# When a batch's rows are scattered: six indirect DMAs of GpSimd moved to later units, in the first two of four batches

## The chip, the cores and the metric

One core of a Trainium2 chip runs the whole program in one launch. The metric is the device time of one execution in microseconds (us), lower is better. The kernel before takes 246.15 us, the median of three runs (246.1 to 246.69).

## The reference, cut to what matters

An attention with selected key chunks over 4 batches of 8 heads, 768 positions and 64 dimensions feeds a mixture of experts: every one of the 3072 rows goes through a dense two-layer network, and through the one of 8 experts that its gate prefers.

```
ub = sum(max(q*k_min, q*k_max))            # bound of each 32-key chunk, causal
top_chunks = argsort(ub)[..., -6:]         # six chunks for each query
scores = where(selected and causal, q@k.T / 8, -1e9)
attn = exp(scores - max); attn /= sum
x = (attn @ v) reshaped to (3072, 512)
y = relu(x @ w1_dense) @ w2_dense
e = argmax(x @ w_gate);  g = softmax(x @ w_gate)[e]
y[rows of e] += g * (relu(x[rows of e] @ w1[e]) @ w2[e])
```

## The kernel before

The attention is worked off in 16 pairs of heads (pair 0 to 15; four pairs are a batch of 768 rows), and each pair in 11 units (unit 0 to 10). A unit is a group of score tiles with up to 512 columns: TensorE multiplies (L604 in `scores`, tile `sp`), ScalarE takes the exponential (L608, tile `ex`), and where the tiles lie on the diagonal, in units 0, 5 and 6, GpSimd zeroes what is not causal with an affine select (L610, called a mask here). TensorE then multiplies `ex` with the values (L623 in `av`, tile `op`). Score tiles have three PSUM buffers.

The main loop `for i, (p, u) in enumerate(seq)` writes in each step: the scores of the unit two steps on, preparations for later pairs, the work of an earlier batch that is due in this step, and the product with the values of the unit before. Preparations are: `prep_k` (k is transposed, ScalarE copies it to `kp`, VectorE reduces it at L546 and makes `kb` at L549), `prep_q`, `prep_kt` (VectorE copies `kp` to `kT`, L553 and L554), `prep_ub` (bounds, and the flags `fl` at L584) and `prep_s` (TensorE transposes the flags at L590, tile `ps`). In unit 0 GpSimd casts v of a later pair (L535) and issues one or two expert weight loads (`we`, L214), in unit 7 it casts k and q (L528, L530).

When a batch of four pairs is done, `batch_fills(b)` lists its routing and its dense layer as small closures, and a table `at` gives each a number n. The closure with number n is run in step n + 1 of the next batch's 44 steps, so n = 0 to 9 falls in its first pair, 10 to 20 in its second, and so on. `ranks` (n = 15) computes on TensorE and VectorE the row `slot` of the table at which each token will lie (L308). `place(t)`, for t = 0 to 5, scatters 128 rows of `xbig` to the DRAM tensor `table` by an indirect DMA which GpSimd issues (L388, called a placing here); the first one also copies the row numbers into `xbig` (L382). `xbig` has two buffers, used by turns by the batches, so VectorE's first normalised rows (L634) of the batch after next wait until the six placings of this one have landed. The expert blocks of the tail read `table` after the attention.

Each engine takes its instructions in the order in which they are queued. A placing is held behind the last mask written before it (`issue_after(latest["pool"].ins)`), and a scheduler settles the rest of the order. Batch 0 is placed during pairs 5 to 7, batch 1 during pairs 9 to 11, batch 2 during pairs 13 to 15, and batch 3 in the tail, where `at` is not used.

Of the kernel before, what the change touches and what calls it, by code (L numbers as in the profile page):

```python
# [17 lines left out]
def kernel(  # L18
# [13 lines left out]
    B, H, S, D = q.shape  # L32
    NT = S // 128
# [220 lines left out]
    def batch_fills(b):  # L254
# [122 lines left out]
        def place(t):  # L377

            def f():
                with tc.issue_after(latest["pool"].ins):  # L380
                    if t == 0:
                        nc.gpsimd.tensor_copy(xbig[b % 2][:, :, Dm + 2 : Dm + 4].bitcast(mybir.dt.int32),  # L382
                                              num[:, b * NT : (b + 1) * NT])
                    put(t)
            return f

        def put(t):
            sc = nc.gpsimd.indirect_dma_start(  # L388
                out=table, out_offset=bass.IndirectOffsetOnAxis(ap=keep["slot"][:, t : t + 1], axis=0),
                in_=xbig[b % 2][:, t].bitcast(U16), in_offset=None)  # L390
            apart(sc, "rows", "every token has a row of its own")
            latest["put"] = sc
            if b == B - 1:
                tc.declare_no_dep(sc.ins, group="full", reason="the first blocks were full before this batch")
# [56 lines left out]
        at = {}  # L451
        for n, f in zip((0, 2, 4, 6, 8, 10) + (12,), out_list):
            at.setdefault(n, []).append(f)
        at.setdefault(15, []).append(ranks)
        for t in range(NT):
            at.setdefault(18 + 3 * t, []).append(place(t))
        for n, f in zip((7, 8, 9, 10, 12, 13, 14, 15, 17, 18, 19, 20, 22, 23, 24, 25, 27, 28, 29, 30, 32, 33, 34, 35, 37, 38, 39, 40), dense):
            at.setdefault(n, []).append(f)
        return out_list, dense, ranks, [place(t) for t in range(NT)], at
# [56 lines left out]
    with (  # L516
# [239 lines left out]
        def finish(p, u):  # L756
            av(p, u)
            for g in range(2):
                if u == done[g]:
                    norm(p, g)  # L760
            if u == NU - 1:
                if p % HP == HP - 1 and p + 1 < NP:
                    fills.clear()
                    fills.update(batch_fills(p // HP)[-1])
# [74 lines left out]
    with (  # L839
# [6 lines left out]
        cur.update(tr=(p1, "tr"), h=(p2, "h"), y=(p3, "y"), rk=(p4, "rk"))  # L846
        assert not fills
        a, d, ranks, places, _ = batch_fills(B - 1)

        w2f = we2.rearrange("p e j f -> p (e j f)")  # L850
# [145 lines left out]
```

## Time and profile before

| | |
|---|---|
| median of three runs | 246.15 us |
| the profiled execution: its time / its span | 247.56 us / 245.9 us |
| attention, from the start to the last masks | about 161 us |
| busy share of the span | TensorE 86%, VectorE 71%, ScalarE 71%, GpSimd 66% |
| mean granted TensorE clock | 0.983 |
| masks (L610) | 48, 667 ns each (median) |
| placings (L388) | 24, 984 ns each (median) |

The profile lists for an engine when each instruction ran, and in brackets how long the engine had stood idle before it and what ended that. [...] A wait put down to "issue" is one whose releaser the profile doesn't show.

### The profile page before, as it was taken

How to read it: one execution, taken by the hardware profiler on the slowest of the kernel's cores; microseconds unless marked ns; L12 is line 12 of the kernel's file. 1: busy time of each engine (PE TensorE's matmuls, PEld its weight loads, DVE VectorE, ACT ScalarE, POOL GpSimd, SP SyncE). 2: the span in 40 equal slices, each digit the busy share in tenths (PEclk: the TensorE clock that was granted, in tenths of full speed). 3: DMA queues.
4: the chain of work that ended last, by engine and by line, in shares of the span. 5: the costliest groups of instructions: out<-in, count | busy, mean ns of one | idle time of the engine just before them, and what ended most of it. 6: DMA issues, size and time to landing. Idle time of an engine off the chain costs nothing.

```text
span 245.9 us, 7890 instructions
## 1 busy us (share of the span) xinstructions
PE 211.6 (86%) x2771; PEld 149.6 (61%) x2771; DVE 175.4 (71%) x561; ACT 174.3 (71%) x325; POOL 162.9 (66%) x213
## 2 busy tenths in 40 slices
PE   1688878898997999988999996989999989999950
PEld 0466556676666676755667764667666557777720
DVE  3889999999989789797798996577723335555510
ACT  4579797897887898696899786644556556666630
POOL 6457997785379687268877517330688757888881
PEclk9999999999999999999999998899999999999996
DMA  6999999999899999979999946147589999968785
GB/s 174 247 268 279 210 240 251 270 214 265 222 168 358 182 300 261 263 128 251 296 177 256 188 82 182 42 119 197 157 267 215 222 250 254 204 130 122 88 122 106
DMA packets 68279, 50.55 MB, mean 206 GB/s; under 512 B 29712, under 2 KB 61328, under 8 KB 68240
## 3 DMA queue, kind: packets, MB, share of 16 engines
q1 hardware_dynamic: 53008, 30.72, 47.0%
q0 software_dynamic: 15232, 19.32, 45.8%
q8 instruction: 23, 0.38, 0.6%
q14 instruction: 16, 0.13, 0.2%
HBM read 41.93 MB, written 18.23 MB: 245 GB/s over the span
## 4 chain that ended last, share of the span: by engine, by line
PE 35%; POOL 16%; DVE 14%; issue 12%; ACT 10%; DMA 10%; POOLq 1%; SPq 0%; DVEq 0%; ACTq 0%
ACT ex L608 6%; PE yp L886 6%; PE hp L865 6%; PE hp L408 5%; POOL ex L610 4%; DMA out_dram<-yo,xg 4%; DVE ks L546 4%; PE sp L604 4%; POOL table L388 4%; PE yp L424 4%; DMA xg<-table 2%; PE op L623 2%; DMA qf<-in_q_dram 2%; ACT kp L543 2%; PE tp L856 2%
## 5 line engine op out<-in xcount | busy, mean ns | idle before, releaser
L608 ACT ACTIVATE ex<-sp 128x512 f16<-128x512 f32 (+1 forms) x176 | 91.5, 613 | 10.3 <-PE sp L604 8.5
L604 PE MATMUL sp<-rT,kT 128*128 128x128 f16 (+3 forms) x384 | 64.3, 262 | 4.3 <-ACT ex L608 1.1
L610 POOL TENSOR_SCALAR_AFFINE_SELECT ex<-ex 128x512 f16<-128x512 f16 x48 | 32.4, 685 | 37.7 <-ACT ex L608 25.6
L895 POOL DMA_INDIRECT out_dram<-yo,xg x27 | 44.8, 1660 | 12.0 <-issue 5.2
L623 PE MATMUL op<-v,ex 128*128 128x65 f16 x672 | 45.9, 194 | 7.2 <-POOL ex L610 5.6
L623 PEld LDWEIGHTS <-ex 128*128 128x128 f16 x672 | 35.9, 98 | 23.1 <-POOL ex L610 10.0
L388 POOL DMA_INDIRECT table<-xbig,slot x24 | 24.3, 1012 | 18.5 <-issue 18.5
L858 DVE COPY exT<-tp 128x512 f16<-128x512 f16 x28 | 11.8, 423 | 32.8 <-PE tp L856 31.5
L604 PEld LDWEIGHTS <-kT 128*128 128x128 f16 x384 | 28.5, 98 | 8.4 <-issue 5.2
L886 PE MATMUL yp<-we,ehT 128*128 x112 | 30.9, 379 | 0.4 <-ACT ys L429 0.2
L865 PEld LDWEIGHTS <-w 128*128 128x128 f16 x432 | 26.4, 98 | 7.9 <-issue 2.2
L408 PE MATMUL hp<-xT,wd 128*128 128x384 f16 x128 | 30.2, 341 | 0.6 <-DVE xT L264 0.6
L865 PE MATMUL hp<-exT,w 128*128 128x128 f16 x432 | 29.2, 219 | 0.7 <-issue 0.7
L893 ACT ACTIVATE yo<-yp,xg 128x512 f32<-128x512 f32 x27 | 18.5, 687 | 14.0 <-PE yp L886 13.2
L546 DVE TENSOR_REDUCE ks<-kp 128x24 f16<-128x768 f16 x28 | 25.5, 945 | 3.7 <-ACT kp L543 3.5
L424 PE MATMUL yp<-wd,hT 128*128 128x512 f16 x96 | 25.7, 379 | 0.3
L868 ACT ACTIVATE ehT<-hp 128x512 f16<-128x512 f32 x28 | 16.7, 597 | 12.1 <-PE hp L865 9.0
L413 ACT ACTIVATE hT<-hp 128x384 f16<-128x384 f32 x30 | 15.0, 498 | 12.0 <-PE hp L408 11.4
L513 DVE COPY w<-we 128x2048 f16 x27 | 18.7, 693 | 0.2 <-DVE exT L858 0.2
L634 DVE TENSOR_TENSOR xbig<-op,rs 128x384 f16<-128x384 f32 x32 | 17.5, 547 | 0.3
L429 ACT COPY ys<-yp 128x512 f32<-128x512 f32 x21 | 12.8, 609 | 6.3 <-PE yp L424 6.0
L886 PEld LDWEIGHTS <-ehT 128*128 128x128 f16 x112 | 10.2, 97 | 10.3 <-issue 3.6
(158 smaller groups left out, 371.6 us busy)
## 6 DMA issues: line engine op xcount, KB each, us to landing
we<-in_moe_w_dram POOLq DMA_DIRECT2D x16, 512.0 KB, 6.6
kf<-in_k_dram SPq DMA_DIRECT2D x32, 192.0 KB
qf<-in_q_dram SPq DMA_DIRECT2D x32, 192.0 KB
vf<-in_v_dram SPq DMA_DIRECT2D x32, 192.0 KB
out_dram<-ys SPq DMA_DIRECT2D x48, 128.0 KB
xg<-table SPq DMA_DIRECT2D x27, 136.0 KB
table<-zt SPq DMA_DIRECT2D x9, 136.0 KB
wd<-in_moe_w_dense_dram POOLq DMA_DIRECT2D x2, 512.0 KB, 6.3
```

Source lines behind the costliest of these rows:

```text
L388: sc = nc.gpsimd.indirect_dma_start(out=table, out_offset=bass.IndirectOffsetOnAxis(ap=keep["slot"][:, t : t + 1], axis=0), in_=xbig[b % 2 ...
L408: nc.tensor.matmul(hp, wd[:, ko, j * 128 : (j + 1) * 128], xT[:, ko, g * G * 128 : (g + 1) * G * 128], start=(ko == 0), stop=(ko == NK - 1))
L424: nc.tensor.matmul(yp, hold["h"][:, j, i * 128 : (i + 1) * 128], wd[:, NK + j], start=(j == 0), stop=(j == NK - 1))
L513: nc.vector.tensor_copy(w.rearrange("p j f -> p (j f)"), w1f[:, bass.ds(offs1[i], NK * 512)])
L546: nc.vector.tensor_reduce(out=ks[:, i], in_=kp.rearrange("d (c w) -> d c w", w=32), op=op, axis=mybir.AxisListType.X)
L604: last = nc.tensor.matmul(sp[:, o : o + w], kT[p % NB][g][:, kt * 128 : (kt + 1) * 128], rT[p % NB][g][:, a * 128 : z * 128], start=(o == ...
L608: scored.append((last, nc.scalar.activation(ex[:, 0:o], sp[:, 0:o], AF.Exp, scale=-0.125)))
L610: latest["pool"] = nc.gpsimd.affine_select(out=ex, in_=ex, compare_op=ALU.is_ge, fill=0.0, base=0, pattern=[[0, 4], [1, 2], [2, 64]], chan ...
L623: nc.tensor.matmul(s["op", g][:, t * (D + 1) : (t + 1) * (D + 1)], ex[:, o : o + 128], v16[p % NB][:, g, kt, :], start=first, stop=(last_o ...
L865: nc.tensor.matmul(hp[:, j], s["w1"][:, ko, j * 128 : (j + 1) * 128], s["xT"][:, ko], start=(ko == 0), stop=(ko == NK - 1), skip_group_che ...
L886: nc.tensor.matmul(yp, s["hT"][:, j], w2f[:, bass.ds(offs[i] + j * 512, 512)], start=(j == 0), stop=(j == NK - 1))
L895: sc = nc.gpsimd.indirect_dma_start(out=out, out_offset=to, in_=o, in_offset=None, bounds_check=N - 1, oob_is_err=False, compute_op=ALU.by ...
```

## The change

In `batch_fills` the placings of the first two batches get the numbers 25, 26, 30, 33, 36 and 37; they had 18, 21, 24, 27, 30 and 33. Batch 2 keeps those, batch 3 was never on the table. Each placing is thus written 4 to 7 units later, and no instruction is added or removed.

```
-        for t in range(NT):
-            at.setdefault(18 + 3 * t, []).append(place(t))
+        for t, n in enumerate((25, 26, 30, 33, 36, 37) if b < B - 2 else range(18, 36, 3)):
+            at.setdefault(n, []).append(place(t))
```

What follows is GpSimd's queue during batch 1's placings, in pair 10, from the two weight loads (`we`) behind the cast of v, to the mask of unit 0 of pair 11. `table<-xbig,slot` is a placing, and the AFFINE_SELECT rows are the masks. Before:

```order
L214 DMA we_176<-in_moe_w2_dram 128x4x512 x2
L388 DMA table<-xbig_172,slot 25728x544 x2
L610 AFFINE_SELECT ex<-ex 128x512
L388 DMA table<-xbig_172,slot 25728x544
L610 AFFINE_SELECT ex<-ex 128x512
L388 DMA table<-xbig_172,slot 25728x544
L528 CAST k_2806<-kf 128x768
L530 CAST q_2808<-qf 128x768
L610 AFFINE_SELECT ex<-ex 128x512
```

And now, for the same stretch:

```order
L214 DMA we_176<-in_moe_w2_dram 128x4x512 x2
L610 AFFINE_SELECT ex<-ex 128x512 x2
L382 COPY xbig_172<-num 128x6
L528 CAST k_2804<-kf 128x768
L388 DMA table<-xbig_172,slot 25728x544 x2
L530 CAST q_2806<-qf 128x768
L610 AFFINE_SELECT ex<-ex 128x512
```

The masks of units 5 and 6 stand ahead of all placings, where three stood ahead of or between them; two placings now stand between the casts of k and q.

The next stretch of the same queue runs from that mask to the mask of unit 0 of pair 12. Before:

```order
L388 DMA table<-xbig_172,slot 25728x544 x2
L535 CAST v_1_119<-vf 128x12x64
L214 DMA we_176<-in_moe_w2_dram 128x4x512 x2
L610 AFFINE_SELECT ex<-ex 128x512 x2
L528 CAST k_3034<-kf 128x768
L530 CAST q_3036<-qf 128x768
L610 AFFINE_SELECT ex<-ex 128x512
```

And now:

```order
L388 DMA table<-xbig_172,slot 25728x544 x2
L535 CAST v_1_119<-vf 128x12x64
L214 DMA we_176<-in_moe_w2_dram 128x4x512 x2
L610 AFFINE_SELECT ex<-ex 128x512 x2
L388 DMA table<-xbig_172,slot 25728x544 x2
L528 CAST k_3034<-kf 128x768
L530 CAST q_3036<-qf 128x768
L610 AFFINE_SELECT ex<-ex 128x512
```

Two more placings stand here, behind the second pair of masks and ahead of the casts. In pairs 6 to 8 the queue changes in the same way for batch 0, with one weight load in place of two. On TensorE, VectorE and ScalarE no instruction moves. On SyncE's queue two stores of dense rows (`ys`) come ahead of two loads of q once, in batch 0.

## Rows read from the trace of the kernel before

**Rows 1.** The page: busy time of each engine, and the chain that ended last by engine.

```profile
PE 211.6 (86%) x2771; PEld 149.6 (61%) x2771; DVE 175.4 (71%) x561; ACT 174.3 (71%) x325; POOL 162.9 (66%) x213
...
PE 35%; POOL 16%; DVE 14%; issue 12%; ACT 10%; DMA 10%; POOLq 1%; SPq 0%; DVEq 0%; ACTq 0%
```

**Rows 2.** Busy time by stretches of 10 us: the stretch, its length, busy us (and instructions) of TensorE, its weight loads, VectorE, ScalarE, GpSimd, then the granted clock, the DMA share and GB/s. Two stretches of the attention and one of the tail.

```profile
110.00:120.00 10.00, 7.83 (x113) 5.72 (x113) 8.03 (x25) 7.86 (x17) 8.47 (x10) 1.00 1.09 284
120.00:130.00 10.00, 9.50 (x140) 6.94 (x138) 7.69 (x26) 8.86 (x19) 8.17 (x12) 1.00 1.04 194
...
220.00:230.00 10.00, 10.00 (x122) 7.59 (x121) 5.22 (x11) 6.42 (x10) 8.48 (x6) 1.00 0.80 120
```

**Rows 3.** Who waited for whom in pair 10, 106 to 122 us: engine and line, releaser, us in total, times, longest.

```profile
POOL table L388 <- issue: 2.8, 6, 1.6
...
PE op L623 <- POOL ex L610: 1.6, 1, 1.6
```

**Rows 4.** GpSimd in order of time, pair 10 to the first mask of pair 12: start, length, instruction, idle before it.

```profile
105.48 1.50 POOL L214 DMA_DIRECT2D we<-in_moe_w_dram  x2
108.62 1.04 POOL L388 DMA_INDIRECT table<-xbig,slot  x1 [1.65 <-issue]
109.96 1.01 POOL L388 DMA_INDIRECT table<-xbig,slot  x1 [0.30 <-issue]
110.99 0.67 POOL L610 TENSOR_SCALAR_AFFINE_SELECT ex<-ex 128x512 f16<-128x512 f16 x1
111.83 0.97 POOL L388 DMA_INDIRECT table<-xbig,slot  x1 [0.18 <-issue]
112.83 0.68 POOL L610 TENSOR_SCALAR_AFFINE_SELECT ex<-ex 128x512 f16<-128x512 f16 x1
...
115.42 0.83 POOL L530 CAST q<-qf 128x768 f16<-128x768 f32 x1
116.92 0.67 POOL L610 TENSOR_SCALAR_AFFINE_SELECT ex<-ex 128x512 f16<-128x512 f16 x1 [0.67 <-ACT ex L608]
...
122.39 1.31 POOL L610 TENSOR_SCALAR_AFFINE_SELECT ex<-ex 128x512 f16<-128x512 f16 x2
...
124.39 0.84 POOL L530 CAST q<-qf 128x768 f16<-128x768 f32 x1
127.05 0.74 POOL L610 TENSOR_SCALAR_AFFINE_SELECT ex<-ex 128x512 f16<-128x512 f16 x1 [1.82 <-ACT ex L608]
```

**Rows 5.** The other engines in the same stretch, in order of time: ScalarE's exponentials of units 4, 5 and 6 of pair 10, the slots, the last score product ahead of the wait, the flags, the product that waited, the transposed flags, and at the start of pair 12 the run of exponentials and the product with its first mask.

```profile
106.74 1.57 ACT L608 ACTIVATE ex<-sp 128x384 f16<-128x384 f32 x3
107.64 0.19 DVE L308 TENSOR_REDUCE slot<-rt 128x6 int32<-128x48 f32 x1
109.71 0.38 PE L604 MATMUL sp<-rT,kT 128*128 128x512 f16 x1
109.89 0.46 DVE L584 TENSOR_TENSOR fl<-ub,m 128x288 f16<-128x288 f32 x1
111.72 0.30 PE L623 MATMUL op<-v,ex 128*128 128x65 f16 x4 [1.62 <-POOL ex L610]
112.01 0.50 PE L590 MATMUL ps<-ident,fl 128*128 128x128 f16 x6
...
126.25 5.12 ACT L608 ACTIVATE ex<-sp 128x512 f16<-128x512 f32 x10
127.84 0.30 PE L623 MATMUL op<-v,ex 128*128 128x65 f16 x4 [0.27 <-POOL ex L610]
```

**Rows 6.** GpSimd in order of time in batch 0's stretch, pairs 6 to 8: the masks of units 5 and 6 of pair 6, of unit 0 of pair 7, of unit 6 of pair 7, and of unit 0 of pair 8.

```profile
70.84 0.68 POOL L610 TENSOR_SCALAR_AFFINE_SELECT ex<-ex 128x512 f16<-128x512 f16 x1
...
72.69 0.68 POOL L610 TENSOR_SCALAR_AFFINE_SELECT ex<-ex 128x512 f16<-128x512 f16 x1
...
76.08 0.67 POOL L610 TENSOR_SCALAR_AFFINE_SELECT ex<-ex 128x512 f16<-128x512 f16 x1
...
82.28 0.67 POOL L610 TENSOR_SCALAR_AFFINE_SELECT ex<-ex 128x512 f16<-128x512 f16 x1 [0.82 <-ACT ex L608]
...
87.02 0.74 POOL L610 TENSOR_SCALAR_AFFINE_SELECT ex<-ex 128x512 f16<-128x512 f16 x1 [2.53 <-DMA vf<-in_v_dram]
```

**Rows 7.** VectorE in order of time: a copy to `kT` beside two masks of pair 5, a `kb` at the end of pair 6, the first normalised rows of pair 8, the two copies to `kT` at the end of pair 11, and the flags that follow them.

```profile
57.34 0.72 DVE L554 COPY kT<-kp 64x768 f16<-64x768 f16 x1
...
75.43 1.38 DVE L549 TENSOR_TENSOR kb<-ks,hmask 128x96 f16<-128x96 f16 x1
...
91.62 0.56 DVE L634 TENSOR_TENSOR xbig<-op,rs 128x384 f16<-128x384 f32 x1
...
126.10 0.31 DVE L553 COPY kT<-kp 64x768 f16<-64x768 f16 x1
...
126.90 0.36 DVE L554 COPY kT<-kp 64x768 f16<-64x768 f16 x1
...
128.33 0.46 DVE L584 TENSOR_TENSOR fl<-ub,m 128x288 f16<-128x288 f32 x1
```

**Rows 8.** TensorE in order of time: the transposes of those flags.

```profile
129.17 0.50 PE L590 MATMUL ps<-ident,fl 128*128 128x128 f16 x6
```

**Rows 9.** All instructions of L549: min/median/max duration in ns, first and last start, forms.

```profile
L549 DVE TENSOR_TENSOR kb<-ks,hmask x14: 197/199/1377, 21.3 to 144.9; 128x96 f16<-128x96 f16 x14
```

**Rows 10.** The 24 placings (L388): time from issue to landing.

```profile
DMA to landing us min/median/max: 2.7/3.4/6.9
```

## The prediction

> **What bounds the kernel now.** I read the page first, then stretches of 10 us, then who waited for whom where batches 0 and 1 are placed, then the engines' own order of time there. The page shows no engine that is full: TensorE 86%, the others 66 to 71%, and a chain that changes engine all the time [rows 1]. So a placing costs something only where its place in GpSimd's queue makes another engine wait. In the stretches, TensorE works 7.83 us of 110 to 120 us and 9.50 us of the next ten [rows 2]: that dip is pair 10, where batch 1 is placed. Its cause is one wait of 1.62 us of the product with the values for a mask; GpSimd itself stood 2.8 us ahead of placings [rows 3].
>
> The order of time shows how that comes about. The weight loads end at 106.98. The next instruction is the first placing, which needs the slots; VectorE writes these from 107.64 to 107.83, and the placing starts at 108.62 [rows 4, 5]. The second follows, and only then, at 110.99, the mask of unit 5, though the exponentials of units 4 to 6 had ended by 108.31 (106.74 + 1.57) [rows 4, 5]. TensorE stops for that mask and goes on at 111.72; VectorE and ScalarE then wait for TensorE. From about 170 us on the tail keeps TensorE busy 10.00 of 10 us [rows 2], so I take it that what the attention gains or loses arrives at the end undiminished.
>
> **Batch 1, pair 10: the wait goes.** Now the masks of units 5 and 6 stand right behind the weight loads. GpSimd is free at 106.98, the inputs are there at about 107.8 and 108.3, a mask takes 0.67 [rows 4]: both are done by about 109.2. TensorE can multiply right behind the score product of 109.71. What is late next is the flags: their transposes began at 112.01 and can't begin before the flags end at 109.89 + 0.46 = 110.35 [rows 5]. So TensorE gains 112.01 - 110.39 = **1.62 us**, the same number as the wait by chance. The mask of unit 6 moves from 112.83 to 108.5; nobody waited for it longer. Two placings (0.97 each, gaps of 0.18 and 0.30 [rows 4]) between the casts of k and q end by about 113.5 with the cast of q, well ahead of the mask of unit 0 of pair 11, which is ready at 116.92 - 1.62 = 115.3. The casts come earlier than before (the cast of q ended at 116.25), so the loads of k and q that SyncE queues behind them are not late.
>
> **Batch 1, pairs 11 and 12: part is given back.** From 115.3 GpSimd has the same work as before up to the masks of units 5 and 6 (two placings, v, two loads), so these end 1.62 earlier than 122.39 + 1.31 = 123.70, at 122.08 [rows 4]. But then two placings more, 0.18 + 0.97 + 0.30 + 0.97 = 2.42, to 124.5. The casts of k and q (1.53 from 123.70 to 125.23) then end at 126.1. The mask of unit 0 of pair 12 would be ready at 127.05 - 1.62 = 125.4, and stands in the queue until 126.1: it is 0.95 earlier than before, not 1.62. Its cover, an idle time of 1.82 us [rows 4], is gone. The product at 127.84 waited 0.27 for this mask already [rows 5], so TensorE has no slack here, and ScalarE's run of ten exponentials [rows 5] is fed by score products that stand behind it. **Given back: 0.67.** If the queue is 0.67 shorter than I reckon, nothing is given back; if it is longer by most of a placing, all is: the bounds are 0 and 1.62.
>
> **VectorE's copies beside GpSimd's casts.** VectorE copies `kp` to `kT` at 126.10 and 126.90, in that idle time [rows 7]. Moved up by 1.62 they fall at 124.5 and 125.3, where GpSimd now runs cast, cast and mask without a gap. The trace shows what that does: a copy that takes 0.36 us at 126.90 took 0.72 beside two masks at 57.34 [rows 7], and a `kb`, 0.20 at the median [rows 9], took 1.38 at 75.43 [rows 7], through the end of one GpSimd instruction and the whole of the next. The flags that follow the copies end at 128.79, their transposes start at 129.17 [rows 7, 8]: 0.38 of slack. In pair 12 the copies may lose 0.67 before they lose what TensorE has given back anyway, and 0.38 more before TensorE notices. I take one GpSimd instruction for each copy at most, some 0.8 together, hidden there. At the end of pair 7 the same two copies meet the same run of GpSimd with no gain in hand; 0.5 of waits less 0.38 of slack is about **0.1 lost**.
>
> [...]
>
> **Batch 0, pairs 6 to 8.** Here there is little to win. The mask of unit 5 starts at 70.84 in any case, and that of unit 6 (72.69) moves up by over a microsecond [rows 6], but TensorE had other work and no wait for either; I take zero. The mask of unit 0 of pair 7 now has two placings and the cast of q ahead of it and starts about 0.3 later than at 76.08; the exponentials behind cover that. The last two placings follow the mask of 82.28: to 82.95, plus 2.42, plus 1.53 is 86.9, and the mask of unit 0 of pair 8 was at 87.02 [rows 6]: just free. One thing is open: the `kb` that lost 1.18 to GpSimd (1.38 - 0.20) wants to run at 75.43, where GpSimd now ends a placing and starts the cast of q. Which is first I can't tell to 0.1 us. It is worth 0 to 1.18, and as GpSimd's queue would then be full from pair 7's first mask up to pair 8's, about 0.55 of it would arrive. I take 0, since either order is as near.
>
> **Landings, stores.** VectorE may not overwrite `xbig` before the placings have landed. The last of batch 0 is now issued at about 84.4; with the longest landing, 6.9 [rows 10], it is down at 91.3, and VectorE writes at 91.62 [rows 7]. Batch 1 has more room. The two stores that now pass two loads of q on SyncE are waited for by nobody near. Both cost nothing, up to 0.5 if a landing is slower than any shown.
>
> **Sum.** -1.62 + 0.67 + 0.1 = -0.85. On the profiled execution that is 247.56 - 0.85 = 246.71 us. That execution is 1.41 above the median of 246.15, so the forecast for the median is **245.3 us**.
>
> **Rivals.** First, the `kb` of pair 6 gets ahead of GpSimd's cast: 0.55 more is won, 244.75. For it: a placing, not a cast, is at work at 75.4. Against it: 0.1 us decides.
>
> Second, it is all given back: GpSimd's queue ahead of pair 12 is longer than reckoned, by 0.6 or more, as placings behind weight loads can be slow to start (the gap of 1.65 is the largest [rows 4]). Then pair 12 starts 0 to 0.3 earlier and batch 0 loses 0.1 to 0.3: 246.0, no change that can be measured.
>
> Third, slower: the copies to `kT` are held through two GpSimd instructions, as the `kb` was. Let h be the hold at each of the two places. At the end of pair 7 it costs h - 0.38; at the end of pair 11 the gain is the smaller of 0.95 and 1.62 + 0.38 - h. The two cancel at h = 1.2. With 1.18 for one copy and 1.18 for the other, h = 2.36: +1.98 in batch 0 and +0.36 in batch 1, 248.5; with 1.18 and 0.36, 246.9. I name 247.4 for it. Against it: one instruction in 14 of L549 shows such a hold [rows 9].
>
> Fourth, the change doesn't do what it says: the scheduler puts the placings elsewhere. The order of instructions shows them behind the masks, so this is as good as excluded, and goes with the second.
>
> **Chances.** Forecast (244.9 to 245.6) 0.45, first 0.15, second 0.28, third 0.12. About 0.3%, or 0.74 us, can be told from no change. The forecast's own range reaches over that line, and I put a sixth of it within: faster 0.37 + 0.15 = 0.52; same 0.08 + 0.26 = 0.34; slower 0.12 + 0.02 = 0.14. Of the second's 0.28, 0.02 lies on the slow side. The range takes in the first rival with nearly the whole 1.18 (244.2) and the second with a slower landing, up to where the third begins: 244.2 to 246.8.
>
> **What would show it.** Right: in pair 10 the masks of units 5 and 6 follow the weight loads with no placing ahead, the wait of 1.62 is gone, and TensorE's dip with it; the mask of unit 0 of pair 12 follows the cast of q without idle time, about 1 us earlier than 127.05. Wrong, if that mask is not earlier; if copies to `kT` at the ends of pairs 7 and 11 take over 1 us; if `kb` in pair 6 takes 0.2; if the norm at 91.62 waits for a DMA; or if pair 13 starts earlier and the tail doesn't.

## The result, and the profile after

The changed kernel is slower: 248.34 us, the median of 22 runs (246.45 to 249.93), where the kernel before took 246.44 on the same chip (22 runs, 245.50 to 248.05). The ratio is 1.0065, with a 95% interval of 1.0044 to 1.0086, so 1.1 to 2.1 us are lost where the prediction had 0.85 gained. The profiled execution took 249.58 us, with a span of 247.9.

The page of the kernel after, busy time by engine and the chain that ended last:

```profile
PE 210.7 (85%) x2771; PEld 149.7 (60%) x2771; DVE 178.3 (72%) x561; ACT 174.9 (71%) x325; POOL 163.4 (66%) x213
...
PE 26%; DVE 24%; DMA 19%; POOL 13%; issue 9%; ACT 5%; SPq 1%; POOLq 1%; DVEq 0%; ACTq 0%
```

Against [rows 1], TensorE is 0.9 us less busy and VectorE 2.9 us more, with the same 561 instructions. VectorE was not given more work, so some of its instructions took longer. In the chain its share rose from 14 to 24%.

To find the place I compared the starts of one recurring VectorE instruction, the normalised rows (L634), in both traces. It stands on the attention's path, twice in each pair. The last column is a second profiled execution of the changed kernel (from the run "after again", below).

| normalised rows (L634) of | before, us | after: start, and against before | again: against before |
|---|---|---|---|
| pair 5, second | 68.67 | 70.85, +2.18 | +0.84 |
| pair 6, second | 79.58 | 81.24, +1.66 | +0.31 |
| pair 7, first | 86.30 | 89.70, +3.40 | +2.06 |
| pair 8, second | 97.43 | 101.24, +3.81 | +2.47 |
| pair 9, second | 108.48 | 112.28, +3.80 | +2.46 |
| pair 10, first | 112.22 | 114.29, +2.07 | +0.73 |
| pair 11, second | 128.71 | 131.16, +2.45 | +1.10 |
| pair 12, first | 135.78 | 139.00, +3.22 | +1.87 |
| pair 14, first | 153.77 | 156.89, +3.12 | +1.77 |
| pair 14, second | 157.93 | 159.53, +1.60 | +0.25 |

Only steps of the difference belong to the change, not the difference itself. The first moved instruction runs in pair 6, so the 2.18 that is there in pair 5 is not of the change (in the second execution it is 0.84). The drop of 1.52 within pair 14 is not of it either: the profiled execution of before had the lower clock there, as its windows of 145 to 155 us show (columns as in [rows 2]),

```profile
145.00:150.00 5.00, 4.08 (x59) 2.70 (x57) 4.88 (x39) 3.92 (x9) 2.65 (x3) 1.00 0.47 118
150.00:155.00 5.00, 3.92 (x26) 2.18 (x27) 3.08 (x8) 2.27 (x5) 2.71 (x4) 0.73 0.52 156
```

with a granted clock of 1.00 in the first 5 us and 0.73 in the second. The execution of after kept 1.00 there:

```profile
150.00:155.00 5.00, 3.20 (x39) 1.87 (x35) 4.01 (x31) 3.87 (x8) 4.25 (x5) 1.00 0.79 207
```

The ten traces of the runs below bear this out. Of them and the trace of after, the eight with 1.00 in those 5 us all show the drop against before, 1.51 or 1.52, whatever their queue; the other three, with 0.66 to 0.93 there, show 0.22 to 0.30.

What is left are five steps, equal to 0.01 in both executions of the changed kernel: **-0.52** in pair 6, **+1.74** between pair 6's and pair 7's rows and +0.40 behind them, **-1.73** in pair 10, and **+1.15** from there to pair 12. The sum is +1.04. The large ones have their rows.

The step of +1.74 is one instruction of VectorE. After, VectorE's two `kb` of batch 0's stretch in order of time,

```profile
77.61 0.30 DVE L549 TENSOR_TENSOR kb<-ks,hmask 128x96 f16<-128x96 f16 x1
...
86.79 1.94 DVE L549 TENSOR_TENSOR kb<-ks,hmask 128x96 f16<-128x96 f16 x1
```

and GpSimd beside the second, from the last two placings of batch 0 to the mask of unit 0 of pair 8:

```profile
84.76 1.01 POOL L388 DMA_INDIRECT table<-xbig,slot  x1 [0.16 <-issue]
86.08 0.97 POOL L388 DMA_INDIRECT table<-xbig,slot  x1 [0.30 <-issue]
87.06 0.82 POOL L528 CAST k<-kf 128x768 f16<-128x768 f32 x1
87.84 0.82 POOL L530 CAST q<-qf 128x768 f16<-128x768 f32 x1
88.67 0.67 POOL L610 TENSOR_SCALAR_AFFINE_SELECT ex<-ex 128x512 f16<-128x512 f16 x1
```

The `kb` of pair 7 ends at 86.79 + 1.94 = 88.73, just behind the end of the cast of q (88.66): it was held through both casts. (Neighbouring records overlap a little: the cast of k ends at 87.06 + 0.82 = 87.88, and that of q starts at 87.84.) Who waited for whom after, 84 to 94 us (us in total, times, longest), shows how TensorE paid, 1.7 us in two waits, for the `kb` and for the flags that VectorE makes behind it:

```profile
PE ub L576 <- DVE kb L549: 1.0, 1, 1.0
...
PE ps L590 <- DVE fl L584: 0.7, 1, 0.7
```

In the kernel before, that `kb` ran while GpSimd stood idle ahead of the mask at 87.02 [rows 6]:

```profile
85.13 0.20 DVE L549 TENSOR_TENSOR kb<-ks,hmask 128x96 f16<-128x96 f16 x1
```

1.94 - 0.20 is the whole step of 1.74, and neither wait is in the trace of before. The step of -0.52 is the same kind of thing with its sign turned: the `kb` of pair 6, 1.38 us in [rows 7], takes 0.30 now, 1.08 less. But the copy to `kT` behind it, which was not held before,

```profile
77.41 0.35 DVE L553 COPY kT<-kp 64x768 f16<-64x768 f16 x1
```

now is, beside the end of the cast of q and the mask behind it:

```profile
78.51 0.91 DVE L553 COPY kT<-kp 64x768 f16<-64x768 f16 x1
```

It takes 0.56 back, and -1.08 + 0.56 is the step.

Pair 10 came as forecast. GpSimd after, from the masks of units 5 and 6, and TensorE's product that had waited 1.62 us in [rows 5]:

```profile
111.71 1.45 POOL L610 TENSOR_SCALAR_AFFINE_SELECT ex<-ex 128x512 f16<-128x512 f16 x2 [0.92 <-ACT ex L608]
113.12 0.19 POOL L382 COPY xbig<-num 128x6 int32<-128x6 int32 x1
113.25 0.82 POOL L528 CAST k<-kf 128x768 f16<-128x768 f32 x1
```

```profile
113.75 0.29 PE L623 MATMUL op<-v,ex 128*128 128x65 f16 x4
```

No wait stands behind it any more, and TensorE works 9.88 us of 110 to 120 us where it worked 7.83 in [rows 2]. Ahead of pair 12, GpSimd's order of time after, from the masks of units 5 and 6 of pair 11, and TensorE's product with that pair's first mask:

```profile
124.60 1.32 POOL L610 TENSOR_SCALAR_AFFINE_SELECT ex<-ex 128x512 f16<-128x512 f16 x2
126.10 1.04 POOL L388 DMA_INDIRECT table<-xbig,slot  x1 [0.18 <-issue]
127.45 1.02 POOL L388 DMA_INDIRECT table<-xbig,slot  x1 [0.30 <-issue]
128.48 1.02 POOL L528 CAST k<-kf 128x768 f16<-128x768 f32 x1
129.45 0.94 POOL L530 CAST q<-qf 128x768 f16<-128x768 f32 x1
130.36 0.66 POOL L610 TENSOR_SCALAR_AFFINE_SELECT ex<-ex 128x512 f16<-128x512 f16 x1
```

```profile
131.07 0.30 PE L623 MATMUL op<-v,ex 128*128 128x65 f16 x4 [1.29 <-POOL ex L610]
```

The idle 1.82 us ahead of this mask [rows 4] is gone, as the prediction said, but the wait of TensorE grew from 0.27 [rows 5] to 1.29.

### The profile page after: what moved, and what is told of

It reads as the page before. It is cut to its first block, busy times and chain, and to the rows that moved or that the text cites. A ratio compares the mean times of both kernels' runs of the same rounds, so it can differ in the third digit from the quotient of the medians.

```text
span 247.9 us, 7892 instructions
## 1 busy us (share of the span) xinstructions
PE 210.7 (85%) x2771; PEld 149.7 (60%) x2771; DVE 178.3 (72%) x561; ACT 174.9 (71%) x325; POOL 163.4 (66%) x213
## 4 chain that ended last, share of the span: by engine, by line
PE 26%; DVE 24%; DMA 19%; POOL 13%; issue 9%; ACT 5%; SPq 1%; POOLq 1%; DVEq 0%; ACTq 0%
DMA out_dram<-yo,xg 7%; DVE ks L546 6%; DMA vf<-in_v_dram 5%; POOL table L388 4%; PE yp L886 4%; PE hp L408 4%; DMA xg<-table 4%; PE hp L865 4%; PE yp L424 3%; POOL ex L610 3%; ACT ex L608 3%; DVE m L582 3%; DMA we<-in_moe_w_dram 2%; PE sp L604 2%; DVE kT L554 2%
## 5 line engine op out<-in xcount | busy, mean ns | idle before, releaser
L388 POOL DMA_INDIRECT table<-xbig,slot x24 | 24.5, 1021 | 16.8 <-issue 16.5
L408 PE MATMUL hp<-xT,wd 128*128 128x384 f16 x128 | 28.6, 325 | 0.6 <-DVE xT L264 0.6
L634 DVE TENSOR_TENSOR xbig<-op,rs 128x384 f16<-128x384 f32 x32 | 17.5, 547 | 0.3
L535 POOL CAST v<-vf 128x768 f16<-128x768 f32 x16 | 13.5, 842 | 5.6 <-PE op L623 4.2
```

The source lines that it names most:

```text
L388: sc = nc.gpsimd.indirect_dma_start(out=table, out_offset=bass.IndirectOffsetOnAxis(ap=keep["slot"][:, t : t + 1], axis=0), in_=xbig[b % 2 ...
L408: nc.tensor.matmul(hp, wd[:, ko, j * 128 : (j + 1) * 128], xT[:, ko, g * G * 128 : (g + 1) * G * 128], start=(ko == 0), stop=(ko == NK - 1))
```

## The experiments

The theory: the loss sits in batch 0 and is the hold of the `kb` of pair 7 by GpSimd's casts, which the last two placings of batch 0 push onto it. The rivals: the loss is GpSimd's longer queue as such, which makes masks late (in either batch); or it is in batch 1, whose gain is given back; or the hold comes from any GpSimd work without a gap, placings too.

Each edit but one (the input from PSUM) replaces the one line of the change; after the first edit only new lines are shown. Below, a number list stands for that line's list, for batch 0 and batch 1; `old` is 18, 21, 24, 27, 30, 33 and `new` is 25, 26, 30, 33, 36, 37. Batches 2 and 3 stay as they were throughout. Shares of the loss are read as above, from the steps of L634, so that they don't hang on the clock of pair 14 or on how an execution began; "batch 0" is from pair 5's second to pair 9's second, "batch 1" from there to pair 12's first. The four runs from "batch 0 only" to "one input from PSUM" shared a chip on which the kernel before takes 253.96 us; "after again" and the three that follow "one input from PSUM" had it at 246.50, the last two at 246.66.

| run | batch 0 / batch 1 | median us | ratio to before, 95% | batch 0, us | batch 1, us | `kb` of pairs 6 and 7, us |
|---|---|---|---|---|---|---|
| before | old / old | | 1 | | | 1.38, 0.20 |
| after again | new / new | 248.28 | 1.0090 (1.0058 to 1.0121) | +1.62 | -0.59 | 0.29, 1.94 |
| batch 0 only | new / old | 255.07 | 1.0042 (1.0008 to 1.0077) | +1.92 | +0.06 | 0.99, 1.93 |
| batch 1 only | old / new | 253.74 | 0.9987 (0.9954 to 1.0021) | +0.56 | -0.07 | 0.20, 0.20 |
| last two behind the casts | 25, 26, 30, 33, 40, 40 / new | 254.26 | 1.0012 (0.9978 to 1.0045) | +1.45 | -0.50 | 0.29, 0.20 |
| one input from PSUM | new / new | 255.50 | 1.0046 (1.0010 to 1.0083) | +2.00 | -0.46 | 0.28, 0.25 |
| last two of batch 0 alone | 18, 21, 24, 27, 36, 37 / old | 249.06 | 1.0112 (1.0076 to 1.0148) | +2.13 | +0.01 | 1.38, 1.93 |
| batch 1 spread | old / 29, 29, 29, 31, 31, 40 | 245.06 | 0.9942 (0.9919 to 0.9965) | +0.01 | -1.18 | 1.40, 0.20 |
| batch 1, tail behind the casts | old / 25, 26, 30, 33, 40, 40 | 246.07 | 0.9984 (0.9957 to 1.0012) | +0.01 | -0.93 | 1.39, 0.20 |
| one placing of batch 0 | 18, 21, 24, 29, 30, 33 / old | 245.41 | 0.9952 (0.9922 to 0.9982) | -0.79 | 0.00 | 0.20, 0.20 |
| that and batch 1 spread | 18, 21, 24, 29, 30, 33 / 29, 29, 29, 31, 31, 40 | 244.51 | 0.9908 (0.9871 to 0.9944) | -0.78 | -1.16 | 0.20, 0.20 |

**Either batch alone.**

```
-        for t, n in enumerate((25, 26, 30, 33, 36, 37) if b < B - 2 else range(18, 36, 3)):
+        for t, n in enumerate((25, 26, 30, 33, 36, 37) if b == 0 else range(18, 36, 3)):
```

> Batch 0 alone has the new numbers; batch 1 has the old ones. Theory (VectorE's small product kb that is made in pair 7 meets a placing and the casts of k and q without a gap, and waits 1.7 us for them): slower than before by 1.5 to 2.4 us, kb of pair 7 over 1.5 us long, pair 10 as before with its wait of 1.6 us for a mask. Rival A (it is not this product, but the mask of the next pair's unit 0 that stands behind placings and casts, alike in both batches): slower by 0.8 to 1.0. Rival B (the loss comes from loads that arrive late by chance, and not from the change): within 0.3%.

Batch 0 only loses 1.92 us, with the `kb` of pair 7 at 1.93. By the medians it is 1.0042, about 1.1 us, which is nearer to rival A than to the theory; what speaks for the theory is the trace, with its step of 1.74 at that `kb`. The `kb` of pair 6 took 0.99 here, through one cast, and 0.29 or 0.30 in the changed kernel, with the same queue, and what decides that is not shown. The same line with `b == 1`:

> Batch 1 alone has the new numbers; batch 0 has the old ones. Theory: faster than before by 0.5 to 1.0 us, the forecast's terms (1.6 won in pair 10, 0.7 to 1.0 given back ahead of pair 12). Rival A: slower by 0.8 to 1.0. Rival B: within 0.3% of the kernel before, either sign.

In batch 1 only, pair 10 gains its 1.73 and nearly all of it is back by pair 12: -0.07 is left, and the 0.5 to 1.0 expected did not come. Of what is given back, 0.78 lies between pair 11's second rows and pair 12's first, as in the changed kernel (0.77); the rest lies in pairs 10 and 11, 0.88 here and 0.38 there, with the same queue, and why is open. (The +0.56 in batch 0's stretch of that run stands in pairs 5 to 7, where its program is that of before: pair 6's first rows came 1.59 later against pair 5's, and its `kb`, later too, met nothing and took 0.20. So such steps can differ by half a microsecond between executions.) Who waited ahead of pair 12 in this run, 122 to 132 us (us in total, times, longest):

```profile
PE op L623 <- POOL ex L610: 1.3, 1, 1.3
```

That is the wait of after, without any change in batch 0. So the give-back is batch 1's own, and the loss is batch 0's.

**The last two placings of batch 0 behind the casts.** With batch 0 at 25, 26, 30, 33, 40, 40, the casts of pair 7 come early again, and the two placings run beside what had been held.

```
+        for t, n in enumerate(((25, 26, 30, 33, 40, 40), (25, 26, 30, 33, 36, 37), range(18, 36, 3), range(18, 36, 3))[b]):
```

> The change, but with the last two placings of batch 0 behind the casts of k and q of pair 7, not ahead of them; batch 1 as changed. Theory: the casts run where they ran before the change, kb of pair 7 is not held by them (0.2 us, or up to 0.5 if a placing holds it too), and 1.5 to 2.0 us of the loss come back: between 0.8 faster than before and 0.3 slower. Rival A: the mask of pair 8's unit 0 stands behind the same instructions, so the time is that of the changed kernel, 1.6 slower than before. Rival B: as the changed kernel.

GpSimd, and VectorE's `kb`, which took 0.20 right beside a placing, and the normalised rows of pair 8:

```profile
84.78 1.01 POOL L388 DMA_INDIRECT table<-xbig,slot  x1 [0.15 <-issue]
```

```profile
85.27 0.20 DVE L549 TENSOR_TENSOR kb<-ks,hmask 128x96 f16<-128x96 f16 x1
...
93.15 0.56 DVE L634 TENSOR_TENSOR xbig<-op,rs 128x384 f16<-128x384 f32 x1 [0.98 <-DMA table<-xbig,slot]
```

The hold is gone, and another wait took its place: VectorE may not overwrite `xbig` until the placings have landed, and the last of them is now late by 0.98. Of the 1.45 lost in batch 0, 1.40 comes between pair 7's first rows (+0.13 against before there) and pair 8's first (+1.53), and 0.98 of that is this wait. So the 1.5 to 2.0 expected did not come back, this placing is no way out, and the time alone, 1.0012, would not have told that the `kb` was free.

**One input of that `kb` from PSUM.** In the changed kernel, the maxima and minima `ks` of pair 9's keys, which the `kb` of pair 7's steps reads, lie in PSUM in place of SBUF, as 32-bit numbers; TensorE's dense products move slightly.

```
+            pk0 = pprep.tile([128, 1024 if p == 9 else S], HF, name="pk", tag="pp"); pk = pk0[:, 0:S]
...
+            ks = pk0[:, 896 : 896 + 4 * NC].bitcast(FP).rearrange("d (i c) -> d i c", i=2) if p == 9 else ahead.tile([128, 2, NC], HF, name="ks")
```

> The change, and for the one pair whose kb is made in pair 7 the reduced keys lie in PSUM, so that kb has one operand in SBUF and one in PSUM; GpSimd's queue is as changed, and some dense products of TensorE change their order. Theory: kb of pair 7 takes 0.2 to 0.3 us beside the placing and the casts, and the time falls by 1.3 to 2.0 against the changed kernel. Rival A: kb may be short, but the time stays that of the changed kernel within 0.4. Rival B: as the changed kernel.

GpSimd had the same queue, placing, cast, cast, mask; VectorE beside it:

```profile
85.13 0.25 DVE L549 TENSOR_TENSOR kb<-pk,hmask 128x96 f16<-128x96 f32 x1
...
86.47 1.99 DVE L553 COPY kT<-kp 64x768 f16<-64x768 f16 x1
```

```profile
85.26 0.82 POOL L528 CAST k<-kf 128x768 f16<-128x768 f32 x1
86.03 0.82 POOL L530 CAST q<-qf 128x768 f16<-128x768 f32 x1
86.80 0.66 POOL L610 TENSOR_SCALAR_AFFINE_SELECT ex<-ex 128x512 f16<-128x512 f16 x1
87.42 0.82 POOL L535 CAST v<-vf 128x768 f16<-128x768 f32 x1
```

With one input in SBUF the `kb` was not held, but the copy to `kT` that follows was, for 1.99, until just after the cast of v (88.24). The loss stays (+2.00), as rival A had it. It is not the `kb` as such that costs: here the copy to `kT` met the unbroken run of GpSimd in its place. That PSUM freed the `kb` is not shown by this one trace, as the `kb` of pair 6, with both inputs in SBUF, got by at 0.28 to 0.30 in four traces, beside a placing and a cast as well.

**The last two alone, and two ways for batch 1.** These shared one chip with a second run of the changed kernel.

```
+        for t, n in enumerate(((18, 21, 24, 27, 36, 37), range(18, 36, 3), range(18, 36, 3), range(18, 36, 3))[b]):
```

> The kernel before, and only the last two placings of batch 0 moved: from ahead of the cast of v in pair 7 to where the change puts them, between the masks of units 5 and 6 of pair 7 and the casts of k and q. Theory: these two carry batch 0's loss; the small product kb of pair 7 is held 1.5 to 2 us by the casts, and the time is 0.8 to 1.9 longer than before. Rival A (the first four placings, or a full queue as such, carry it): within 0.4 of before, kb of pair 7 0.2 us.

Two placings of batch 0, moved by themselves, lose 2.13 us (by the medians 1.9 to 3.6, where 0.8 to 1.9 was expected), 1.73 of it from pair 6's second rows (+0.32) to pair 7's first (+2.05) with `kb` at 1.93:

```profile
85.45 1.93 DVE L549 TENSOR_TENSOR kb<-ks,hmask 128x96 f16<-128x96 f16 x1
```

```profile
84.73 0.97 POOL L388 DMA_INDIRECT table<-xbig,slot  x1 [0.31 <-issue]
85.71 0.83 POOL L528 CAST k<-kf 128x768 f16<-128x768 f32 x1
86.49 0.82 POOL L530 CAST q<-qf 128x768 f16<-128x768 f32 x1
87.34 0.66 POOL L610 TENSOR_SCALAR_AFFINE_SELECT ex<-ex 128x512 f16<-128x512 f16 x1
```

The mask behind this queue is at 87.34, where the kernel before has it at 87.02 [rows 6]: it is late by no more than the 0.32 with which this execution came. So the longer queue of GpSimd is not what costs here; the held VectorE is. For batch 1, three placings behind pair 10's casts, two ahead of the cast of v and one behind pair 11's casts, so that none stands ahead of casts:

```
+        for t, n in enumerate((range(18, 36, 3), (29, 29, 29, 31, 31, 40), range(18, 36, 3), range(18, 36, 3))[b]):
```

> Batch 0 as before; batch 1 with numbers 29, 29, 29, 31, 31, 40: three placings behind the casts of pair 10, two ahead of the cast of v in pair 11, one behind the casts of pair 11. Theory: the 1.7 of pair 10 are won as in the change, the casts run where they ran before, and only one placing stands ahead of the mask of pair 12's unit 0, in time that was idle; so 1.0 to 1.7 faster than before, and the product with that mask waits under 0.5 us. Rival (what is won in pair 10 is taken back by VectorE and ScalarE in pairs 11 and 12, whatever the queue): as batch 1 alone with the changed numbers, 0.5 faster to 0.1 slower.

This beat both kernels: 245.06 us, 0.9942. GpSimd ahead of pair 12's first mask, idle again for 0.61:

```profile
123.16 0.85 POOL L530 CAST q<-qf 128x768 f16<-128x768 f32 x1
124.18 1.04 POOL L388 DMA_INDIRECT table<-xbig,slot  x1 [0.18 <-issue]
125.83 0.66 POOL L610 TENSOR_SCALAR_AFFINE_SELECT ex<-ex 128x512 f16<-128x512 f16 x1 [0.61 <-ACT ex L608]
```

TensorE's waits for masks at 122 to 132 us fall from 1.3 to

```profile
PE op L623 <- POOL ex L610: 0.2, 1, 0.2
```

and 1.18 of pair 10's 1.73 are kept. Where only the last two placings of `new` go behind pair 11's casts (25, 26, 30, 33, 40, 40 for batch 1),

> Batch 0 as before; batch 1 with the change's numbers for four placings, and the last two behind the casts of k and q of pair 11, not ahead of them. Theory: two placings (2.4 us) still stand ahead of the mask of pair 12's unit 0, so 0.5 to 0.9 are given back there, but VectorE's copies to kT no longer meet two casts: 0.6 to 1.2 faster than before. Rival: as batch 1 alone with the changed numbers, 0.5 faster to 0.1 slower.

0.93 is kept by the rows; by the medians, 0.9984 with an interval that holds 1, nothing is shown. The changed kernel once more:

> The changed kernel once more, for a second trace. Theory: kb of pair 7 is held over 1.5 us again, pair 10 gains about 1.7, the product with the first mask of pair 12 waits over 1 us, and the time is 0.8 to 2.1 longer than before. Rival B (chance): kb of pair 7 takes 0.2 this time, and the time is within 0.3% of before.

Its steps are those of the first trace, and the interval of 1.0090 overlaps that of 1.0065.

**The hold taken away where it was from the start.** The kernel before has one such hold itself, the `kb` of pair 6 at 75.43, 1.38 us [rows 7]. If it is GpSimd's casts that hold it, moving one placing from ahead of pair 6's casts to behind them should free it, although GpSimd is then no less busy.

```
+        for t, n in enumerate(((18, 21, 24, 29, 30, 33), range(18, 36, 3), range(18, 36, 3), range(18, 36, 3))[b]):
```

> The kernel before with one placing of batch 0 moved: the fourth goes from ahead of pair 6's casts of k and q to behind them (numbers 18, 21, 24, 29, 30, 33); all else stays. Theory of the hold: the casts then end near 75.1 us, ahead of the kb of pair 6, which in the kernel before meets both and takes 1.38 us; it takes 0.20 beside the placing, TensorE's wait of 1.23 for it goes, and 0.5 to 1.2 us is gained; the median ratio is 0.995 to 0.998. Rival (the hold comes from any queue of GpSimd without a gap, placings too): kb still takes 1 us or more beside the placing, and the time is that of the kernel before, 0.999 to 1.003, since the mask of pair 7's unit 0 starts about 0.3 later.

```profile
73.87 0.83 POOL L530 CAST q<-qf 128x768 f16<-128x768 f32 x1
74.86 0.98 POOL L388 DMA_INDIRECT table<-xbig,slot  x1 [0.17 <-issue]
```

```profile
75.21 0.20 DVE L549 TENSOR_TENSOR kb<-ks,hmask 128x96 f16<-128x96 f16 x1
76.01 0.74 DVE L553 COPY kT<-kp 64x768 f16<-64x768 f16 x1
```

The first fence is GpSimd, the second VectorE. The `kb` takes 0.20 beside the placing, and 0.79 is gained in pair 6 (0.9952 by the medians). The next copy pays 0.74 beside a mask, where it took 0.35 before: 1.18 less 0.39 is the gain. With both:

> The same one placing of batch 0 moved, and batch 1 with numbers 29, 29, 29, 31, 31 and 40 as in the run that beat both kernels. If the two gains add, the ratio to the kernel before is 0.989 to 0.992 (some 243.8 to 244.6 us where the kernel before takes 246.5), with kb of pair 6 at 0.20 and no wait of TensorE for a mask in pair 10. If the attention's gains are taken back by the rows that VectorE or the loads bring later, it stays at 0.994.

The gains add: 244.51 us, 0.9908, the fastest version here.

## Why the prediction was wrong, point by point

**The step that failed** is the part "Batch 0, pairs 6 to 8", with the words "Here there is little to win" and, for the last two placings, "just free". It asked whether GpSimd is done in time for the mask of pair 8, and that was right: the mask is no later than the rest. But the same sum put the casts of k and q at about 85.4 to 86.9, and the prediction did not ask what VectorE does in that time. It looked at the `kb` of pair 6 and at the copies to `kT`; the `kb` of pair 7, at 85.13 in the kernel before, was not among its rows. It met the two casts and paid 1.74, and nothing behind it on the path had slack: the step arrived in full. To have asked would have raised the doubt, not settled it: by the prediction's times this `kb` starts 0.24 ahead of the casts (85.13 and 85.37), and in four traces it started 0.26 to 0.28 ahead of the cast's record and was held all the same.

**Two terms on batch 0.** The `kb` of pair 6 was taken as zero with bounds of 0 and 1.18. It fell to 0.30, and 0.52 arrived, so the first rival happened. That this is nearly the size that it named (0.55) is luck: it let the rest be lost to a full queue from pair 7's first mask on, but the rest was lost before that, to the copy at 78.51. "About 0.1 lost" for the copies at the end of pair 7 is too small: they took 0.31 and 0.66 (0.31 and 0.36 before), which is 0.30. The 0.5 of waits in it was an estimate, under "one GpSimd instruction for each copy at most", and no run shows such a limit: with one input from PSUM, a copy to `kT` took 1.99 in place of 0.31, beside the end of a cast, a mask and another cast. By pair 8's first rows 0.33 was won back; then 0.44 was lost with the copies of pair 8, which the prediction did not look at: 0.64 and 0.85 (0.59 and 0.36 before). These three make up the step of +0.40.

**The third rival** had the right mechanism, a hold through two GpSimd instructions, and the right sign. It put it on the copies to `kT` and at 12%. (The `kb` that it took as its model met more than "the end of one": the cast of q ran from 75.30 to 76.13, so it waited for nearly all of that and for the mask.) Its argument against itself, one instruction in 14 of L549 held, was a count of the long holds in the old queue, and [rows 9] gives only the largest: in the same trace two more `kb`, at 21.27 and 29.40, took 0.36 and 0.80 beside a cast. And it says nothing about a queue that the change fills. This is the first thing that I would do otherwise: the chance of a hold is read from what stands beside the instruction after the change, not from how often it happened before.

**Pair 10:** forecast -1.62, measured -1.73 or -1.74 in every run in which batch 1 was moved. Right, in mechanism and size.

**Given back ahead of pair 12:** forecast 0.67 within 0 and 1.62; measured 1.15. The mechanism was right, the size low. In the changed kernel the mask of unit 0 ran at 130.36, in an execution that was 3.81 late at pair 9, so at 126.55 on the clock of before, where the forecast had 126.1 (126.03 before rounding). The masks of units 5 and 6 ended at 125.92, which is 122.11 on that clock, as forecast (122.08). The 0.5 came behind them: the casts of k and q took 1.88 together (128.48 to 130.36), not 1.53, and the placings with their gaps 2.56, not 2.42.

**Landings and the tail:** right. In the changed kernel VectorE stood idle ahead of none of its 32 normalised rows (L634), so none waited for a placing to land, though the run with numbers 40, 40 shows how near the limit is. From the last normalised rows to the end of the span it was 81.3 us before and 81.7 and 81.5 after, so what the attention lost did arrive. (The reason given is a little too strong: before, TensorE is busy 9.33 to 10.00 of each 10 us from 170 to 230, not always 10.00.)

**The sum:** -0.85 was forecast. By the steps it is -0.52 + 1.74 + 0.40 - 1.73 + 1.15 = +1.04; by the medians 1.1 to 2.1 us, and 1.4 to 3.0 in the second comparison. For the other runs the steps lie within the interval of the medians or at its edge (batch 0 only: 1.98 against 0.2 to 1.96). For the changed kernel they fall a little short, and this stays open: part may be how the executions begin, as both of its profiled executions came later to pair 5 than before's, by 2.18 and 0.84, with identical instructions up to there. In both, GpSimd's cast of q near 46 us waited for its load (0.98 and 0.84 us), and the `kb` beside that cast took 0.85 and 0.72; in the ten other traces the cast did not wait and the `kb` took 0.21. So a part of that delay is the same kind of hold. Another part may be the clock: of the 22 executions of the changed kernel, the eight with a mean granted clock of 0.984 or less took 248.5 to 249.9 us, and the median of the other 14 is 247.7.

Why a cast of GpSimd holds VectorE, and which of its instructions it can hold, no run here shows; what they show is the lengths. One cast took 0.82, and the `kb` 1.94 through two of them; with one input in PSUM it took 0.25, in one trace.

## What to carry to other kernels

When a change fills GpSimd's idle time, list what VectorE does in that time, instruction by instruction, at the new times, and not only who waits for GpSimd's results; where two starts come out as near as here (0.24 us), reckon with both outcomes, held and free. Where small VectorE instructions on the path recur, try GpSimd's DMA issues beside them and its casts and masks elsewhere: here, where a placing was moved from ahead of two casts to behind them, the held instruction went from 1.38 to 0.20 us; the limit on the other side was the landing, 0.98 us late where the placing came too far back. And compare two traces by the steps of one recurring instruction, not by their spans: a span here also held 2.18 and 1.52 us that were not of the change.

## What the hardware did that was not expected

- A VectorE instruction was held through two or three GpSimd instructions that follow each other without a gap, and not only through one: `kb` 0.20 to 1.93 or 1.94 in four traces (two casts), a copy to `kT` 0.31 to 1.99 (the cast under way, a mask and another cast). Each ended within 0.25 us of the end of the last of them. The hold need not last for the whole run: in the changed kernel a mask follows the two casts without a gap, at 88.67, and the `kb` (to 88.73) got in ahead of its end.
- The same `kb` took 0.20 in the middle of a placing, twice (84.78 to 85.79 in one run, 74.86 to 75.84 in another). There an indirect DMA that GpSimd issued did not hold it, where two casts held it to 1.93 or 1.94.
- The held `kb` of the changed kernel has its start at 86.79, 0.27 ahead of the recorded start of the cast at 87.06. The `kb` of pair 6 started only 0.09 ahead of a cast (77.61 and 77.70), and took 0.30. So the starts in the records don't tell whether the `kb` is held, and what decides it is open.
- The kernel before took 246.4 to 246.7 us in three of the comparisons and 253.96 in the other, on another chip, so only ratios from one chip were compared. In the traces the extra lies in the tail: from the last normalised rows to the end it is 86.8 to 88.4 us on that chip and 81.0 to 81.7 in the eight other traces.
